# Pooled attention and top-1 experts on one core: softmax guard as a constant column, eleven route steps spread out in place of sixteen, seven low halves on VectorE

## The chip, the cores and the metric

The kernel runs on one core of a Trainium2 chip. The metric is device time in microseconds (us), the median of the runs. Before the change three runs gave 508.53, 511.44 and 512.01 us: median 511.44.

## What is computed

Attention over pooled keys and values, then a mixture of experts on its output. Everything is float32; batch B = 8, heads H = 8, sequence S = 576, head width 64, so 4,608 tokens of width 512; 8 experts of hidden width 1,024.

```python
def attention(q, k, v):                                  # [8, 8, 576, 64] each
    k_p = k.reshape(B, H, 72, 8, D).mean(axis=3)
    v_p = v.reshape(B, H, 72, 8, D).mean(axis=3)
    scores = 1/sqrt(D) * matmul(q, k_p.transpose(0, 1, 3, 2))
    attn = exp(scores - max(scores, axis=-1, keepdims=True))
    attn = attn / (sum(attn, axis=-1, keepdims=True) + 1e-09)
    return matmul(attn, v_p)

def moe(x, w_skip, w_gate, w1, w2):                      # x: [4608, 512]
    out = x.copy()
    xc = x[x @ w_skip > 0]                               # the other tokens keep x
    logits = xc @ w_gate
    e_idx = argmax(logits, axis=1)
    probs = exp(logits - max(logits)); probs /= sum(probs) + 1e-09
    for e in range(8):
        mask = e_idx == e
        out[those tokens] = xc[mask] + gate_w[mask] * (relu(xc[mask] @ w1[e]) @ w2[e])
    return out
```

## The kernel before

**Stages.** The function attention() works through the 36 tiles of 128 tokens in one loop, and while it does so also routes the tokens to their experts. Each token's gate and number go into a table in DRAM that is sorted by expert. slots() reads this table back, and experts() then gathers each expert's tokens, multiplies and writes them. Products are made with float32 split in a high and a low half (hi x hi, lo x hi, hi x lo), for weights as for tokens: ScalarE (ACT) makes a high half (line 558), GpSimd (POOL) the low half as the difference (line 561, 512 columns).

**One tile.** TensorE (PE) makes the scores of two halves of the heads (72 pooled keys for each head), VectorE (DVE) the least (line 279; keys are kept with a negative sign), ACT the exponentials e (line 285), in the next step of the loop PE turns e in five transposes (lines 292 and 293), ACT copies them (line 297), and one step later PE multiplies by the pooled values (lines 310 and 313). A batch's 72 keys of 8 heads don't fill 128 partitions evenly, so 56 or 72 rows of each head go through four transposes, and what is left of all heads, 4 x 16 rows, through the fifth (line 293), against the small value tile vl4 (64 partitions used). The values have 74 columns: 64 of the head, 9 of the values times the gate weights (so that the logits come out of the same matmul), and a column of ones that gives the sum of e. normalised() then takes the tile: line 325 adds 1e-9 to the sum and multiplies by 8, line 327 inverts, line 331 scales the nine logit columns of each head, line 332 scales the values to x, which goes to the output, and line 335 adds the logits over heads into lg. A batch changes every 4.5 tiles. The new batch's keys are added up on DVE (line 185) and its values on POOL (lines 210 to 241), and at the tiles 5, 9, 13, 18, 22, 27 and 31 PE turns the new values: the "turn tiles".

**The route.** After 9, 14, 18, 24, 29, 33 and 36 tiles route() takes the tiles of that group. It is a generator whose steps are DVE instructions on all the group's tiles at once: maximum (353), no token (355), equal (357), difference (359), times expert number (361), maximum (363), plus "no" (365), one-hot r_oh (367). PE then counts, for each token, those before it of the same expert ("ranks", in the PSUM bank mb), ACT takes the exponentials of the differences (371; 378 in the last group), and DVE adds the running offsets (380), picks by the one-hot (381 and 382), adds up and inverts the gates (383 to 385) and makes the row numbers r_di (390). POOL then writes one row per token and tile into the table (line 393, an indirect DMA). After the first group pick() chooses the expert that has most tokens, which is worked on first; after the third, near_tokens() makes the numbers of its first 256 tokens, which are gathered to SBUF (tile ring; line 468) and multiplied by its weights in 48 small product steps during the end of attention and the table's read (lines 507 to 509 and 529 to 531). That expert's weights come in eight chunks during the loop, from tile 15 on.

**What sets the order.** The order in each engine is written out by the program. normal() runs normalised() and takes one route step behind each of its first two instructions. At the end of a tile, queues with budgets are served: dve holds the key sums (0.7 each), act the high halves, and then route steps are taken while DVE's account stays under 1.5, each counted as 0.13. gps serves POOL: low halves (1.25) and table writes (1.27), with work of at least 1.2 between two writes while there is any. Behind the loop normal() runs for the last tiles, the last group's route runs with product steps of the near tokens put between (side()), and slots() computes the experts' places (s_ names), reads the table (line 956), has PE turn the rows and DVE copy them (lines 987 and 988). WROWS is the time that this planner sets for the table's read. The table is filled with "no token" by one DMA from the tile none (line 734) long before.

Of the kernel before, what the change touches and what calls it, by code (L numbers as in the profile page):

```python
# [56 lines left out]
DVE = 1.5  # L57
GPS = 3.2
# [3 lines left out]
WROWS = 3.6  # L62
# [15 lines left out]
KL = SP - KO  # L78

# [20 lines left out]
def emit(tc, q, k, vm, vr, wg, w1, w2, cf, out):  # L100
    nc = tc.nc
    with ExitStack() as top:
# [10 lines left out]
                 pair=cfs[:, 445 + UNITS:].rearrange("p (g h) -> p g h", h=2), next=cfs[:, 445:445 + UNITS], left=cfs[0:4 * KL, 439:443])  # L113
# [14 lines left out]
        none = cp.tile([128, 266], F32, name="none")  # L128
# [20 lines left out]
def attention(tc, nc, q, k, vm, vr, cf, wg, w1, w2, whi, wlo, out, c, pay, offs, table, near, bufs, late, early, mb, fin, cfs):  # L149
    with ExitStack() as ctx:  # L150
# [7 lines left out]
        n4 = 4 * KL  # L158
# [10 lines left out]
        lg = sp.tile([128, NT, 9], F32, name="lg")  # L169
        wide = [sp.tile([128, 128], F32, name=f"ls{i}") for i in range(2)]  # L170
# [21 lines left out]
        def load_v(b):  # L192
# [3 lines left out]
            vl = vp.tile([n4, POOL, HD], F32, name="vl")  # L196
# [4 lines left out]
            nc.sync.dma_start(vl, vr[b])  # L201
# [79 lines left out]
        def exped(e, sc, mn, i):  # L281
            ev = e[:, i].rearrange("p (k g) -> p g k", g=2)
# [5 lines left out]
        def turn_p(e):  # L288
            for i in range(2):
                ev = e[:, i, 2 * KL * i:2 * KL * i + 256].rearrange("p (k g) -> p g k", g=2)  # L290
                for g in range(2):
                    nc.tensor.transpose(ptf[:, (2 * i + g) * 128:(2 * i + g) * 128 + 128], ev[:, g], ident)
            nc.tensor.transpose(ptf[:, 512:640], e.rearrange("p i k -> p (i k)")[:, 256:384], ident)
# [22 lines left out]
        def normalised(t, os):  # L316
            x = ap.tile([128, H, HD], F32, name="x", bufs=5)
            l8 = ap.tile([128, H, 9], F32, name="l8")
            rs = ap.tile([128, 2, 4], F32, name="rs")
# [14 lines left out]
            yield  # L334
# [5 lines left out]
        def route(t0, n):  # L340
# [6 lines left out]
            cube = lambda i: work[:, (4 + i * NE) * GMAX:(4 + i * NE) * GMAX + n * NE].rearrange("p (j e) -> p j e", e=NE)  # L347
            mx, no, se = (col(i) for i in range(3))
            eq, d = (cube(i) for i in range(2))
            r8 = eq  # L350
            cm = new("r_cm"); c2 = new("r_c2"); oh = new("r_oh", NE, dt=BF16)
            ex = new("r_ex", NE); ds = new("r_ds"); di = new("r_di", dt=I32, bufs=4); s2 = new("r_s2")
# [1114 lines left out]
```

## Time and profile before

| | |
|---|---|
| runs: median, lowest, highest | 511.44, 508.53, 512.01 us |
| profiled execution: its own time | 514.2 us |
| its span (first to last instruction) | 512.4 us |
| PE matmuls busy | 476.5 us, 93% of the span |
| PE weight loads busy (beside matmuls) | 431.9 us, 84% |
| DVE busy | 293.6 us, 57% |
| ACT busy | 233.2 us, 46% |
| POOL busy | 218.9 us, 43% |
| moved by DMA | 88.43 MB, mean 173 GB/s |
| granted clock of PE, mean | 0.98 of full speed |

Span and shares are those of the profiled execution, which took 2.8 us longer than the median of the runs. The shares are averages over stages that differ: the setup and key sums (to 38.77 us), the attention loop (to 152.13), the last route and the table's read (to 189.15), and the experts (to the end). A table by stage, or by tile within a stage, says more than the shares. In a timeline each row has start, length, engine, line and operation, the tile written and the tiles read, the shape, and in brackets the idle time of the engine before it with what ended it.

### The profile page before, as it was taken

The numbers are of one execution on the slowest core, as the hardware profiler recorded it, in microseconds if no ns is written. First come the engines' busy times: TensorE is split into PE (matmuls) and PEld (weight loads), VectorE is DVE, ScalarE is ACT, GpSimd is POOL, SyncE is SP. The second block draws the span as 40 slices with busy tenths as digits, with TensorE's granted clock in tenths as the row PEclk, the third lists the DMA queues.
The fourth block names the chain that finished last, engine by engine and source line by source line (L and its number), as shares of the span: only waits on it lengthen the run. The fifth ranks groups of instructions, "written<-read, shape, count | busy, mean of one in ns | idle before, by whom it ended". The sixth has DMA issues, their size and how long they took to land. (4 is left out here: it accounts for less than half of the span.)

```text
span 512.4 us, 10426 instructions
## 1 busy us (share of the span) xinstructions
PE 476.5 (93%) x3155; PEld 431.9 (84%) x3156; DVE 293.6 (57%) x751; ACT 233.2 (46%) x585; POOL 218.9 (43%) x275
## 2 busy tenths in 40 slices
PE   5899899999998598899999998899999999999994
PEld 2789898898898378788989987789899898989893
DVE  4678988988777333468474747752536644222311
ACT  4677678888881012246343626531434442212110
POOL 3578389999984231034302223442032233223221
PEclk9699999999999899999999999999999999999998
DMA  8999899978311039527572555752335111201001
GB/s 255 395 398 378 323 316 375 343 294 265 108 67 43 25 108 340 187 72 262 182 240 93 179 196 175 264 167 73 89 135 173 61 61 36 67 21 58 30 11 39
DMA packets 35364, 88.43 MB, mean 173 GB/s; under 512 B 6770, under 2 KB 9262, under 8 KB 33508
## 3 DMA queue, kind: packets, MB, share of 16 engines
q1 hardware_dynamic: 27104, 71.62, 39.8%
q0 software_dynamic: 8224, 16.39, 9.5%
q8 instruction: 15, 0.25, 0.2%
q14 instruction: 21, 0.17, 0.1%
HBM read 73.58 MB, written 22.05 MB: 187 GB/s over the span
## 5 line engine op out<-in xcount | busy, mean ns | idle before, releaser
L1196 PE MATMUL psl<-xhi,w1hi 128*128 128x256 f32 (+3 forms) x384 | 112.9, 294 | 3.4 <-PEq L1024 2.8
L1197 PE MATMUL psl<-xlo,w1hi 128*128 128x256 f32 (+3 forms) x384 | 112.4, 293 | 0.0
L1198 PE MATMUL psl<-xhi,w1lo 128*128 128x256 f32 (+3 forms) x384 | 112.4, 293 | 0.0
L1111 POOL DMA_INDIRECT out<-ring,slot x36 | 38.3, 1064 | 162.0 <-POOLq L1024 155.7
L1297 ACT ACTIVATE hhi<-psl 128x256 fp32r<-128x256 f32 (+3 forms) x96 | 39.3, 409 | 119.5 <-ACTq L1024 114.8
L1355 DVE SCALAR_TENSOR_TENSOR hlo<-psl,hhi 128x256 fp32r<-128x256 f32 (+2 forms) x96 | 40.4, 422 | 66.4 <-DVEq L1024 61.7
L1196 PEld LDWEIGHTS psl<-xhi,w1hi 128*128 128x128 f32 x384 | 72.1, 188 | 5.1 <-issue 4.7
L1197 PEld LDWEIGHTS psl<-xlo,w1hi 128*128 128x128 f32 x384 | 72.2, 188 | 0.4
L1198 PEld LDWEIGHTS psl<-xhi,w1lo 128*128 128x128 f32 x384 | 72.1, 188 | 0.0
L285 ACT ACTIVATE e<-sc,mn 128x72 f32<-128x72 f32 x288 | 65.1, 342 | 14.5 <-DVE mn L279 14.3
L1287 ACT ACTIVATE xhi<-psd 128x512 fp32r<-128x512 f32 x36 | 19.1, 597 | 80.2 <-ACTq L1024 79.0
L1106 POOL DMA_INDIRECT ring<-out,slot x39 | 42.2, 1083 | 22.6 <-issue 19.0
L310 PE MATMUL o<-vbd,pT 128*128 128x148 f32 (+1 forms) x312 | 49.4, 298 | 2.6 <-DVE x L332 1.6
L393 POOL DMA_INDIRECT table<-pay,r_di x36 | 35.9, 996 | 17.8 <-DVE p_mx L419 7.5
L310 PEld LDWEIGHTS o<-vbd,pT 128*128 128x128 f32 (+1 forms) x312 | 38.6, 179 | 5.6 <-PE mb L376 1.3
L1218 PE MATMUL psf<-w2hi,hhi 128*128 128x512 f32 x96 | 38.0, 396 | 3.4 <-PEq L1024 3.4
L1332 DVE TENSOR_TENSOR w2lo<-stage,w2hi 128x1024 fp32r<-128x1024 f32 x28 | 34.3, 1224 | 8.6 <-DVEq L1024 8.0
L1219 PE MATMUL psf<-w2lo,hhi 128*128 128x512 f32 x96 | 37.4, 390 | 0.0
L1220 PE MATMUL psf<-w2hi,hlo 128*128 128x512 f32 x96 | 37.4, 390 | 0.0
L1105 POOL COPY ring<-gate 128x1 f32<-128x1 f32 x36 | 10.6, 295 | 56.3 <-DMA out<-ring,slot 49.2
L1218 PE MATMUL mb<-w2hi,hhi 128*128 128x512 f32 x88 | 34.3, 390 | 0.0
L1220 PE MATMUL mb<-w2hi,hlo 128*128 128x512 f32 x88 | 34.3, 390 | 0.0
(240 smaller groups left out, 987.9 us busy)
## 6 DMA issues: line engine op xcount, KB each, us to landing
stage<-in_w SPq DMA_DIRECT2D x64, 512.0 KB, 3.7
out<-x SPq DMA_DIRECT2D x36, 256.0 KB
stage<-in_k SPq DMA_DIRECT2D x7, 1152.0 KB
qt<-in_q SPq DMA_DIRECT2D x9, 512.0 KB
hhi<-in_vm SPq DMA_DIRECT2D x4, 1024.0 KB
hlo<-in_vm SPq DMA_DIRECT2D x3, 1024.0 KB
table<-none POOLq DMA_DIRECT2D x1, 2304.0 KB
xhi<-in_q SPq DMA_DIRECT2D x4, 512.0 KB
```

The lines of the kernel that those rows point to most:

```text
L285: nc.scalar.activation(ev[:, h // 2, k0:k0 + SP], sc[:, h * SP:(h + 1) * SP], AF.Exp, bias=mn[:, 4 * i + h:4 * i + h + 1], scale=-1.0)
L310: nc.tensor.matmul(o_[sl, g * 2 * VA:(g + 1) * 2 * VA], pT[:, 2 * a + g, sl], vbd[b % 2][:, 2 * a + g, :], start=(g == 0), stop=False)
L1106: g.indirect_dma_start(ring[:, s % 6, 0:D], None, out, bass.IndirectOffsetOnAxis(ap=slot[:, s:s + 1], axis=0), bounds_check=NTOK - 1, oob_ ...
L1111: g.indirect_dma_start(out, bass.IndirectOffsetOnAxis(ap=offsets, axis=0), ring[:, s % 6, 0:D], None, bounds_check=NTOK - 1, oob_is_err=Fa ...
L1196: t.matmul(ps, whi[0][:, k, w], xhi[:, k, xs], start=(k == 0), stop=False)
L1197: t.matmul(ps, whi[0][:, k, w], xlo[:, k, xs], start=False, stop=False)
L1198: last = t.matmul(ps, wlo[0][:, k, w], xhi[:, k, xs], start=False, stop=(k == 3))
L1218: t.matmul(ps, hhi[:, k, sl], whi[1][:, k, :], start=(k == 0), stop=False)
L1219: t.matmul(ps, hhi[:, k, sl], wlo[1][:, k, :], start=False, stop=False)
L1220: last = t.matmul(ps, hlo[:, k, sl], whi[1][:, k, :], start=False, stop=(k == 7))
L1297: a.activation(hhi[:, f, xs], psL[f % 3][:, xs], AF.Relu).then_inc(sem["act"], 1)
L1355: return v.scalar_tensor_tensor(out[:, f, :], psL[f % 3][:, xs], 0.0, hhi[:, f, xs].bitcast(F32), ALU.max, ALU.subtract)
```

## The change

**The guard.** Each e tile gets 32 more columns between its two halves; the first of them holds 1.0 and the others 0. The fifth transpose takes the columns 256 to 383 as before, so the constant comes out as one row of the turned tile, and the small value tile has 96 used partitions in place of 64, with the value 1e-9 in the sum's column at that row. pair and left, which fill the sum's columns, are multiplied by 8. The sum then comes out of the matmul as 8 (sum + 1e-9), and line 325 is left out of normalised(). The tiles e, vl and ex (the route's exponentials) are fixed buffers, set once by DVE memsets before the loop; the rows of vl come in two DMAs.

**The route.** The one-hot takes six steps in place of eight: equal and times expert number are one scalar_tensor_tensor, and "no" stands in a ninth column of the same tile, so that the maximum takes it in. The running offsets are put into the ranks by a matmul of the identity with offs (line 372), and the copy of the counts back to offs replaces the add. Multiplying by the one-hot and one maximum over nine columns, which makes r_di, replace four steps. The exponentials have a ninth column that holds 1e-9. A step is now counted as 0.24, and from tile 15 on DVE's account for route steps ends at 1.0. In the last group the exponential stands ahead of the ReLU of the near tokens' products on ACT.

**Low halves and the rest.** Of the first expert's sixteen low halves, the second halves of chunks 2 to 6 are made by DVE in the loop (0.65 on its account), and both of chunk 7 by DVE behind the last hidden halves of the near tokens. pick() and near_tokens() take offs and subtract the experts' first rows. The one-element add of line 450 is gone. WROWS is 5.2 in place of 3.6, and the table's fill takes 128 columns of none in place of 256.

```diff
+DVEL = 1.0
...
-WROWS = 3.6
+WROWS = 5.2
...
+GAP = 2 * KL
...
+ebuf = [sp.tile([128, 8 * SP + GAP], F32, name=f"e{i}") for i in range(2)]
+vls = [sp.tile([n4, POOL, HD], F32, name=f"vl{i}") for i in range(2)]
+exps = [sp.tile([128, GMAX, NE + 1], F32, name=f"ex{i}") for i in range(2)]
...
-            nc.sync.dma_start(vl, vr[b])
+            for i in range(2):
+                nc.sync.dma_start(vl[i * 2 * GAP:i * 2 * GAP + GAP], vr[b, i * GAP:i * GAP + GAP])
...
-                nc.vector.tensor_scalar(rs[:, i * n:i * n + n], o[:, :, :, VA - 1], 1e-9, float(POOL), ALU.add, ALU.mult)
-            yield
-            nc.vector.reciprocal(rc, rs)
+                nc.vector.reciprocal(rc[:, i * n:i * n + n], o[:, :, :, VA - 1])
...
-            nc.vector.tensor_tensor(eq, l, bc(mx), ALU.is_equal)
-            yield
             nc.vector.tensor_tensor(d, l, bc(mx), ALU.subtract)
             yield
-            nc.vector.tensor_tensor(eq, eq, epos.unsqueeze(1).broadcast_to([128, n, NE]), ALU.mult)
-            yield
-            nc.vector.tensor_reduce(cm, eq, axis=AX.X, op=ALU.max)
-            yield
-            nc.vector.tensor_tensor(c2, cm, no, ALU.add)
-            yield
-            nc.vector.tensor_tensor(oh, eq, bc(c2), ALU.is_equal)
+            nc.vector.scalar_tensor_tensor(eq, d, 0.0, epos.unsqueeze(1).broadcast_to([128, n, NE]), ALU.is_equal, ALU.mult)
+            yield
+            nc.vector.tensor_reduce(cm, full, axis=AX.X, op=ALU.max)
+            yield
+            nc.vector.tensor_tensor(oh, eq, bc(cm), ALU.is_equal)
             yield NEXT
...
+            nc.tensor.matmul(pr, ident, offs.unsqueeze(1).broadcast_to([128, n + 1, NE]), start=True, stop=False)
...
-            ranked = [lambda: nc.vector.tensor_tensor(r8, pr[:, 0:n], offs.unsqueeze(1).broadcast_to([128, n, NE]), ALU.add),
-                      lambda: nc.vector.tensor_tensor(r8, r8, oh, ALU.mult),
-                      lambda: nc.vector.tensor_reduce(ds, r8, axis=AX.X, op=ALU.add)]
+            ranked = [lambda: nc.vector.tensor_tensor(eq, pr[:, 0:n], oh, ALU.mult),
+                      lambda: nc.vector.tensor_reduce(di, full, axis=AX.X, op=ALU.max)]
             paid = [lambda: nc.vector.tensor_reduce(se, ex, axis=AX.X, op=ALU.add),
-                    lambda: nc.vector.tensor_scalar(s2, se, 1e-9, None, ALU.add),
-                    lambda: nc.vector.reciprocal(pay[:, t0:t0 + n, 1], s2)]
+                    lambda: nc.vector.reciprocal(pay[:, t0:t0 + n, 1], se)]
...
-            nc.vector.tensor_tensor(offs, offs, pr[:, n], ALU.add)
+            fin["counts"] = pr[:, n]
+            if not last:
+                yield
+                nc.vector.tensor_copy(offs, pr[:, n])
...
+        def low_v(cc, i):
+            nc.vector.tensor_tensor(piece(wlo, cc, i), stage[:, room(cc), i * 512:i * 512 + 512],
+                                    piece(whi, cc, i).bitcast(F32), ALU.subtract)
...
         def later_low(cc, i):
+            if cc == 7:
+                return
+            if cc > 1 and i:
+                dve.add(now["t"] + 1, now["t"] + 2, 0.65, lambda: low_v(cc, i))
+                return
             gps.add(now["t"] + 1, (NT if cc > 5 else wload(cc + 3)) - 1, 1.25, lambda: low(cc, i))
...
-                nc.gpsimd.tensor_copy(vbd[i][:, :, (hh + 1) * VA - 1], pair[:, :, hh])
-            nc.gpsimd.tensor_copy(vl4[i][0:n4, :, VA - 1], left)
+                nc.gpsimd.tensor_scalar(vbd[i][:, :, (hh + 1) * VA - 1], pair[:, :, hh], float(POOL), None, ALU.mult)
+            nc.gpsimd.tensor_scalar(vl4[i][0:n4, :, VA - 1], left, float(POOL), None, ALU.mult)
...
-            while t < NT - 1 and busy < DVE and routes.step():
-                busy += 0.13
+            while t < NT - 1 and busy < (DVE if t < PICKED else DVEL) and routes.step():
+                busy += 0.24
...
                 held = kinds(nc.scalar, fin["nti"])
+                for i in range(2):
+                    low_v(7, i)
```

VectorE before, where the second group's route (five tiles) begins in the loop: mn is the least score of a tile, kp the new batch's keys, mb the PSUM bank that also holds the route's work columns.

```order
L185 TENSOR_REDUCE kp<-stage 128x72
L353 TENSOR_REDUCE mb<-lg 128x5
L355 TENSOR_SCALAR mb<-lg 128x5
L357 TENSOR_TENSOR mb<-lg,mb 128x40
L359 TENSOR_TENSOR mb<-lg,mb 128x40
L361 TENSOR_TENSOR mb<-mb,cfs 128x40
L363 TENSOR_REDUCE r_cm<-mb 128x5
L365 TENSOR_TENSOR r_c_1103<-r_cm,mb 128x5
L325 TENSOR_SCALAR rs<-o 128x8
L367 TENSOR_TENSOR r_oh<-mb,r_c_1103 128x40
L327 RECIPROCAL rc<-rs 128x8
```

VectorE after, from the same key sum on (lines 285, 331, 335, 336 and 338 are 279, 327, 331, 332 and 335 of before).

```order
L190 TENSOR_REDUCE kp<-stage 128x72
L356 TENSOR_REDUCE mb<-lg 128x5
L358 TENSOR_SCALAR mb<-lg 128x5
L331 RECIPROCAL rc<-o 128x8
L360 TENSOR_TENSOR mb<-lg,mb 128x40
L335 TENSOR_TENSOR l_1077<-o,rc 128x72
L336 TENSOR_TENSOR x<-o,rc 128x512
L338 TENSOR_REDUCE lg<-l_1077 128x9
L362 SCALAR_TENSOR_TENSOR mb<-mb,cfs 128x5x8
L285 TENSOR_REDUCE mn<-sc 128x4 x2
L190 TENSOR_REDUCE kp<-stage 128x72
L364 TENSOR_REDUCE r_cm<-mb 128x5
```

Of the steps to the one-hot, two stand at the tile's end now, one inside the next tile's normalised(), one behind it and the fifth a tile later, where the first seven of eight stood in a row.

GpSimd before, at the end of the loop and behind it: w2lo is a low half of the first expert's second weights, "table" with r_di a table write, and the last row the table's read (its first rows repeat for some writes ahead of these).

```order
L561 TENSOR_TENSOR w2lo<-stage,w2hi 128x512
L393 DMA table<-pay,r_di 36864x16
L561 TENSOR_TENSOR w2lo<-stage,w2hi 128x512
L393 DMA table<-pay,r_di 36864x16 x9
L956 DMA stage<-table,s_coli 81x2048
```

GpSimd after, at the same place (lines 562, 390 and 974 are 561, 393 and 956 of before; the memset of stage was elsewhere before).

```order
L562 TENSOR_TENSOR w2lo<-stage,w2hi 128x512
L390 DMA table<-pay,r_di 36864x16
L755 MEMSET stage 81x128x2
L390 DMA table<-pay,r_di 36864x16
L562 TENSOR_TENSOR w2lo<-stage,w2hi 128x512
L390 DMA table<-pay,r_di 36864x16 x15
L974 DMA stage<-table,s_coli 81x2048
```

Fifteen writes stand in a row now where nine did, with fewer low halves between the others.

ACT before, behind the loop, where the last group's exponential is (r_ex; lines 837 and 515 make rows of the near tokens' hidden halves).

```order
L837 ACTIVATE hhi<-cfs 128x8x128
L837 ACTIVATE hlo<-cfs 128x8x128
L515 ACTIVATE hhi<-sc 128x2x256
L378 ACTIVATE r_ex<-mb 128x24
L515 ACTIVATE hhi<-pt 128x2x256 x2
```

ACT after, the same place.

```order
L853 ACTIVATE hhi<-cfs 128x8x128
L853 ACTIVATE hlo<-cfs 128x8x128
L378 ACTIVATE ex_130<-mb 128x3x8
L516 ACTIVATE hhi<-sc 128x2x256
L516 ACTIVATE hhi<-pt 128x2x256 x2
```

The exponential of the last group moves ahead of the first hidden half.

## Rows read from the trace of the kernel before

**Rows 1.** Table of two stages: us, busy by engine (instructions), PE clock, DMA share, GB/s
```profile
38.77:152.13 113.36, 109.00 (x912) 102.39 (x911) 97.75 (x357) 92.72 (x307) 95.35 (x105) 1.00 0.78 278
...
189.15:512.40 323.25, 307.72 (x1888) 280.09 (x1888) 153.66 (x259) 113.42 (x190) 87.88 (x107) 0.99 0.38 129
```

**Rows 2.** The same table, between starts of line 332's x on VectorE
```profile
45.36:49.94 4.58, 4.47 (x36) 4.14 (x35) 3.25 (x11) 3.22 (x11) 4.24 (x7) 1.00 1.02 407
...
49.94:53.15 3.21, 3.21 (x27) 3.12 (x26) 2.78 (x10) 2.51 (x9) 0.80 (x1) 1.00 1.07 415
...
53.15:57.60 4.45, 4.16 (x33) 3.87 (x32) 4.21 (x17) 3.47 (x12) 0.24 (x1) 1.00 0.99 394
...
57.60:63.14 5.54, 4.39 (x46) 3.86 (x45) 5.09 (x29) 3.63 (x12) 2.21 (x2) 1.00 0.78 279
...
72.81:77.05 4.24, 4.24 (x35) 4.04 (x34) 4.00 (x17) 3.23 (x12) 2.83 (x4) 1.00 1.01 333
...
88.05:92.23 4.18, 4.18 (x34) 3.87 (x33) 3.94 (x17) 3.88 (x13) 3.82 (x5) 1.00 1.04 401
...
92.23:97.16 4.93, 4.37 (x44) 3.93 (x42) 4.66 (x20) 3.84 (x13) 4.55 (x5) 1.00 1.02 351
...
110.20:119.33 9.13, 8.73 (x74) 8.21 (x72) 8.26 (x35) 7.53 (x25) 8.55 (x14) 1.00 0.59 190
...
128.96:137.54 8.58, 8.49 (x78) 7.88 (x77) 7.23 (x33) 7.14 (x24) 7.92 (x7) 1.00 0.40 124
...
144.14:148.86 4.72, 4.66 (x36) 4.21 (x34) 4.26 (x17) 4.20 (x15) 4.35 (x5) 1.00 0.16 58
```

**Rows 3.** VectorE's timeline in one route burst: start, length, idle before in brackets
```profile
147.30 0.20 DVE L359 TENSOR_TENSOR mb<-lg,mb 128x32 f32<-128x32 f32 x1
147.53 0.20 DVE L361 TENSOR_TENSOR mb<-mb,cfs 128x32 f32<-128x32 f32 x1
...
148.29 0.15 DVE L325 TENSOR_SCALAR rs<-o 128x8 f32<-128x8 f32 x1
148.47 0.20 DVE L327 RECIPROCAL rc<-rs 128x8 f32<-128x8 f32 x1
```

**Rows 4.** Timeline of four engines behind the loop
```profile
156.95 0.18 DVE L367 TENSOR_TENSOR r_oh<-mb,r_c 128x24 bf16<-128x24 f32 x1
...
157.26 0.17 PE L376 MATMUL mb<-r_oh,upper 128*128 128x24 bf16 x1
...
159.50 0.19 ACT L378 ACTIVATE r_ex<-mb 128x24 f32<-128x24 f32 x1
...
159.72 0.19 DVE L380 TENSOR_TENSOR mb<-mb,offs 128x24 f32<-128x24 f32 x1 [2.59 <-ACT r_ex L378]
...
160.79 0.16 DVE L390 TENSOR_TENSOR r_di<-r_ds,mb 128x3 int32<-128x3 f32 x1
...
161.23 0.97 POOL L393 DMA_INDIRECT table<-pay,r_di  x1 [3.56 <-DVE s_n L909]
...
168.40 1.18 POOL L956 DMA_INDIRECT stage<-table,s_coli  x1 [3.65 <-DVE s_last L975]
...
174.63 0.24 DVE L988 CAST slot<-o 128x81 int32<-128x81 f32 x1 [3.44 <-PE o L987]
```

**Rows 5.** Line groups of TensorE in the loop: busy us, mean ns, idle before
```profile
L248 PE MATMUL mb<-wgs,vT 128*128 128x36 f32 x36 | 5.1, 282 | 0.8 <-DVE njt L439 0.8
```

**Rows 6.** Line groups: VectorE's nearest subtraction, GpSimd's low halves (ns minimum/median/maximum)
```profile
L501 DVE TENSOR_TENSOR xlo<-sc,xhi 128x512 fp32r<-128x512 f32 x2 | 1.4, 684 | 0.0
...
L561 POOL TENSOR_TENSOR w2lo<-stage,w2hi x8: 1269/1289/1307, 128.8 to 148.8; 128x512 fp32r<-128x512 f32 x8
```

**Rows 7.** Timeline of GpSimd and VectorE around the one-element add
```profile
95.35 1.28 POOL L561 TENSOR_TENSOR w1lo<-stage,w1hi 128x512 fp32r<-128x512 f32 x1
...
95.45 1.20 DVE L450 TENSOR_TENSOR ncount<-p_cm,p_mx 128x1 f32<-128x1 f32 x1
```

**Rows 8.** GpSimd's timeline: the first table write
```profile
60.91 1.10 POOL L393 DMA_INDIRECT table<-pay,r_di  x1 [7.52 <-DVE p_mx L419]
```

More of the change, by code (lines that the diff above doesn't have):

```diff
@@ L112, in emit @@
         c = dict(ident=cfs[:, 0:128], epos=cfs[:, 384:392], first=cfs[:, 392:400], unit=cfs[:, 436:437], place=cfs[:, 443:444], third=cfs[:, 444:445], wgs=wgs,
-                 pair=cfs[:, 445 + UNITS:].rearrange("p (g h) -> p g h", h=2), next=cfs[:, 445:445 + UNITS], left=cfs[0:4 * KL, 439:443])
+                 pair=cfs[:, 445 + UNITS:].rearrange("p (g h) -> p g h", h=2), next=cfs[:, 445:445 + UNITS], left=cfs[0:4 * KL + GAP, 439:443])
         c["lower"] = cp.tile([128, 128], BF16, name="upper")
@@ L126, in emit @@
                     order=cp.tile([128, NE + 1], I32, name="norder"))
[L128 removed]
+        none = cp.tile([128, 138], F32, name="none")
         stage = cp.tile([128, NST, F], F32, name="stage")
@@ L195, in load_v @@
                 early("room1", 128, 8)
-            vl = vp.tile([n4, POOL, HD], F32, name="vl")
+            vl = vls[b % 2]
             for i in range(2) if b == 0 else ():
@@ L346, in route @@
             col = lambda i: work[:, i * GMAX:i * GMAX + n]
[L347 to L352, printed above, removed]
+            mx, se = (col(i) for i in range(2))
+            full = work[:, 2 * GMAX:2 * GMAX + n * (NE + 1)].rearrange("p (j e) -> p j e", e=NE + 1)
+            eq, no = full[:, :, 0:NE], full[:, :, NE]
+            d = work[:, (3 + NE) * GMAX:(3 + NE) * GMAX + n * NE].rearrange("p (j e) -> p j e", e=NE)
+            cm = new("r_cm"); oh = new("r_oh", NE, dt=BF16); di = new("r_di", dt=I32, bufs=4)
+            ex = exps[list(ends).index(t0 + n) % 2][:, :n]
             nc.vector.tensor_reduce(mx, l, axis=AX.X, op=ALU.max)
@@ L389, in route @@
                 yield
-            nc.vector.tensor_tensor(di, ds, no, ALU.add)
             def write(j):
@@ L440, in pick, with near_tokens @@
             yield
-        def near_tokens(cnt):
+        def near_tokens(ends):
             less = sp.tile([128, 1], F32, name="less")
             nn = sp.tile([128, 1], F32, name="nn")
-            nc.vector.tensor_tensor(p_own, cnt, near["hot"], ALU.mult)
+            nc.vector.tensor_tensor(p_own, ends, c["first"], ALU.subtract)
             yield
-            nc.vector.tensor_reduce(p_cm, p_own, axis=AX.X, op=ALU.add)
+            nc.vector.tensor_tensor(p_own, p_own, near["hot"], ALU.mult)
             yield
-            nc.vector.tensor_tensor(near["count"], p_cm, p_mx, ALU.add)
+            nc.vector.tensor_reduce(near["count"], p_own, axis=AX.X, op=ALU.add)
             yield
@@ L692, in attention @@
             nc.gpsimd.memset(t_, 0.0)
+        for e, vl in zip(ebuf, vls):
+            nc.vector.memset(e[:, 4 * SP:4 * SP + GAP], 0.0)
+            nc.vector.memset(e[:, 4 * SP:4 * SP + 1], 1.0)
+            nc.vector.memset(vl[GAP:2 * GAP], 0.0)
+        for e in exps:
+            nc.vector.memset(e[:, :, NE], 1e-9)
         nc.scalar.activation(near["count"], init[:, 0:1], AF.Exp, scale=0.0)
@@ L757, in normal @@
             routes.step()
-            next(nrm)
+            finish(nrm)
             routes.step()
-            finish(nrm)
             add_routes(t + 1)
@@ L795, in attention @@
             spent = act.take(t, 0.4 if new is not None else 0.0, 1) if t else 0.0
-            es[t] = ap.tile([128, 2, 4 * SP], F32, name="e")
+            es[t] = ebuf[t % 2]
             for i in range(2):
@@ L908, in slots @@
     nc.vector.memset(zero, 0.0)
-    nc.vector.tensor_tensor(n, offs, c["first"], ALU.subtract)
+    nc.vector.tensor_tensor(n, fin["counts"], c["first"], ALU.subtract)
     yield
```

34 lines of the change are left out of this document (18 added, 16 removed).

## The prediction

> **What bounds the kernel now.** I read the table of stages first [rows 1]. The experts fill 323 of 512.4 us with TensorE (PE) busy 307.7, and the change leaves their instructions as they are; what can move is the attention loop (113.4 us in this row) and the 37 us between its end at 152.13 and the experts' first unit at 189.15. In the loop PE, VectorE (DVE), ScalarE (ACT) and GpSimd (POOL) are each busy 82% or more, so shares tell nothing, and I cut it at the starts of DVE's instruction x (line 332), one per tile of 128 tokens [rows 2]. A plain tile takes 3.21 us: PE busy all of it, DVE 2.78. A tile in which a new batch's values are turned takes 4.58 with DVE at 3.25: 1.37 us that DVE doesn't cause. Tiles with route steps are longer: 4.45, 5.54, 4.24, 4.18, 4.93 us, and there DVE's instructions fill the interval while PE shows gaps (4.16 of 4.45, 4.39 of 5.54, 4.37 of 4.93). The route comes as a burst: step starts stand 0.23 us apart (147.30, 147.53) [rows 3], and up to twelve stand in one tile. So PE sets the pace of plain tiles, DVE that of route tiles.
>
> What the eight rows with route steps hold above 3.21 per tile, and above another 1.37 where a turn is in them (5.54, 4.93, 9.13 for two tiles, 8.58 for two), is 1.24 + 0.96 + 1.03 + 0.97 + 0.35 + 1.34 + 0.79 + 1.51 = 8.2 us. That is the most the loop can give by relieving DVE.
>
> Behind the loop a chain sets the end [rows 4]: last group's one-hot (156.95), its ranks on PE (157.26) and exponentials on ACT (159.50), indices (160.79), three table writes on POOL (from 161.23), the read of the table (168.40) that waits for them, and DVE's copy of its rows (174.63). POOL stood idle 3.56 us before those writes, done with the 33 before them at 157.67, so its backlog isn't in this chain.
>
> **Part by part, against the profiled 514.2 us (span 512.4).** The three runs' median is 511.44, so I scale the result by 511.44/514.2.
>
> *Guard through the constant column.* One DVE instruction per tile goes (line 325): about 0.2 us by the starts 148.29 and 148.47 [rows 3]. No matmul is added: the column rides in the leftover transpose, whose tile keeps its 128 columns. The small value tile grows from 64 to 96 partitions at the same elements per partition, which I cost at nothing; the memsets stand ahead of DVE's first data.
>
> *Eleven route steps in place of sixteen, and spread.* I multiplied out DVE's rows between two x of the changed order with the spacings of the trace (0.23 a step, 0.2 less per tile). The first group's two tiles need 3.7 and 3.5, later groups 3.2 per tile with 10 instructions, one tile in which a low half falls 3.5, the tile of the first ring transposes 4.4 (14 instructions). Above 3.21 that leaves 0.5 + 0.3 + 0.1 + 0.3 + 1.2 = 2.4 us of the 8.2; in turning tiles DVE stays under 4.58. Gain 5.8. The upper bound is 8.2; the lower is what PE visibly stood idle in those rows, 0.29 + 1.15 + 0.56 + 0.40 + 0.09 + 0.06 = 2.5. I take 5.8, since PE's ends are modelled and DVE's sums match the lengths.
>
> *Offsets through TensorE.* Each route gains a float32 matmul pair of 80 columns or fewer (line 372) in place of an add. The nearest row is a 36-column float32 matmul: 5.1 us for 36, 0.14 each [rows 5]; two passes in six looped groups are 1.7 us. Nothing if it falls into a PE gap, 1.7 if PE sets the pace everywhere: I take 0.9.
>
> *Seven low halves.* POOL loses seven of 1.28 us, DVE gains seven of about 0.68 (by the nearest DVE subtraction of that size) [rows 6]. Two stand behind the last hidden halves, before DVE waits 3.44 us for the table's rows [rows 4], and are hidden. Five are in the loop; their 0.6 is already in the DVE sums. New is that they read two SBUF tensors while POOL reads SBUF. The trace has one such meeting in the loop: a DVE add of one element took 1.20 us, where small steps take 0.15 to 0.2 [rows 3], and ended as a POOL low half ended [rows 7]. (The change removes that add.) So each may wait 0 to 1.28 us; I take 0.6 on average, 0.4 at the three where DVE has no slack: 1.2, between 0 and 5 x 1.28 = 6.4.
>
> [...]
>
> POOL afterwards: first write about 1.3 us earlier (the first group's indices by the sums above), seven halves at 1.24 us of spacing gone, 1.3 more for writes that now stand next to each other. The 33rd write would end at 157.67 - 1.3 - 8.7 + 1.3 = 149, 152 if each of five DVE halves holds POOL up. The last group's indices come near 155, so fifteen writes in a row stay hidden by 3 us or more. Had the seven halves stayed, POOL would end near 156.4 and its last three writes would be late by 1 us: that is what moving them buys here.
>
> *Table fill of 512-byte rows in place of 1 KB.* POOL stood idle 7.52 us before its first table write [rows 8], so some microseconds more in making or landing the fill are covered.
>
> *Tail.* Before the last indices DVE loses one guard step (0.2), two steps before the one-hot (0.4) and, net, two behind the ranks (0.4): 1.0 us. The 2.59 us between the one-hot and the next DVE step are odd: PE's ranks are recorded done at 157.43, yet ACT's exponential, which DVE waited for, starts at 159.50 [rows 4]. Before, ACT has a ReLU of the near-token products ahead of it; in the changed order the exponential comes first. Between 0 and 2.0 may go; I take 1.0. Behind the indices all waits are the same, and the experts too. WROWS changes nothing: in both orders 36 of 48 product steps precede the table's transposes, the limit.
>
> Sum: 5.8 - 0.9 - 1.2 + 1.0 + 1.0 = 5.7 us; 514.2 - 5.7 = 508.5, scaled 505.8 us.
>
> **Rivals.**
> 1. *PE paces it all.* Rows such as 4.18 us with PE busy 4.18 speak for it; that PE has 27 matmuls in a plain tile's row and only seven more in that one, most of them small, speaks against. The loop gives 2.5 and pays 0.9 and 1.2: 514.2 - 2.4 = 511.8, scaled 509.0 us.
> 2. *Both waits vanish.* The halves meet no POOL read that matters, and the last exponential is prompt: 5.8 - 0.9 + 1.0 + 2.0 = 7.9 us less, scaled 503.6. For it: the new ACT order; against: [rows 7].
> 3. *The halves starve (slower).* If POOL's next read takes the interface again each time, a half on DVE waits not for one POOL instruction but until POOL issues a write. The changed order has one run of about 12 us without a write (from the sixth w1 half left on POOL to the near-token gathers), and two of the five halves fall at it. Waiting 6 us each, they cost 12 in place of 0.8: 514.2 - 5.7 + 11.2 = 519.7, scaled 516.9. It decides the sign from 6.9 us of extra waiting on. Against it: the one-element add got in after a single POOL instruction; but a write, not a read, came next there.
>
> **How the numbers follow.** Forecast 0.55, rival 1 0.18, rival 2 0.19, rival 3 0.08. A measurement of this kernel can tell about 1% from no change; 1% below 511.44 is 506.3. The forecast's own range, 503.5 to 508, lies about two thirds below that: 0.55 x 0.68 + 0.19 = 0.56 faster; rival 3 and a little of rival 1, 0.09 slower; 0.35 within 1%. The range for eight in ten is 501 (all bounds but one good) to 510.5 (rival 1 with dear halves).
>
> **What would show it.** Right: intervals between two x with route steps near 3.2 to 3.5 us, no tile but the first ring tile above 4.6, the last x of the loop near 148.5 us in place of 152.13, POOL idle before the last three writes. DVE's five 512-column halves between 0.68 and 1.9 us long. Wrong: intervals as long as before with PE busy in them (rival 1), a DVE half of 3 us or more (rival 3), a last group's first write that starts where the twelfth of the row ends (POOL bound after all), or an expert stage that isn't 323 us.

## The result and the profile after

The changed kernel takes 506.01 us (503.58 to 508.87, 14 runs), the kernel before 511.46 us (508.53 to 513.77, 14 runs) on the same chip: a ratio of 0.9901, 95% interval 0.988 to 0.9923. The forecast was 505.8. The profiled execution has a span of 504.2 us, with PE busy 475.2, DVE 288.5, ACT 232.8 and POOL 212.8.

The table of stages between starts of x, now line 336, in the columns of [rows 1]. The first two rows are a turn tile and a plain one, the last is the first ring tile (the first that also turns gathered tokens), and the others hold route steps.

```profile
44.34:48.92 4.58, 4.52 (x37) 4.14 (x36) 3.09 (x11) 3.23 (x11) 3.63 (x6) 1.00 1.02 387
48.92:52.13 3.21, 3.21 (x28) 3.12 (x27) 2.64 (x9) 2.53 (x9) 0.60 (x1) 1.00 1.05 359
...
55.64:59.72 4.08, 3.59 (x37) 3.38 (x37) 3.48 (x18) 3.31 (x12) 0.75 (x1) 1.00 1.02 411
...
77.36:82.83 5.47, 5.15 (x45) 4.62 (x44) 3.46 (x15) 4.06 (x13) 5.11 (x7) 1.00 1.02 379
92.45:97.87 5.42, 5.11 (x52) 4.56 (x51) 3.44 (x15) 4.05 (x13) 5.20 (x6) 1.00 1.04 416
97.87:102.30 4.43, 4.34 (x35) 4.03 (x33) 4.39 (x12) 3.91 (x12) 4.07 (x5) 1.00 0.86 320
116.49:120.42 3.93, 3.93 (x38) 3.74 (x37) 3.70 (x12) 3.03 (x11) 3.85 (x6) 1.00 0.56 194
141.73:146.64 4.91, 4.84 (x38) 4.39 (x36) 4.36 (x15) 4.40 (x15) 3.69 (x5) 1.00 0.17 58
```

Against [rows 2]: plain and turn tiles are as long as before, and the bursts of 4.2 to 5.5 us are gone. But two turn tiles now last 5.47 and 5.42 us, one tile 4.43 with DVE busy throughout, and one 3.93 with PE busy throughout.

The timeline behind the loop, the counterpart of [rows 4]:

```profile
153.11 0.18 DVE L366 TENSOR_TENSOR r_oh<-mb,r_cm 128x24 bf16<-128x24 f32 x1
...
153.67 0.17 PE L376 MATMUL mb<-r_oh,upper 128*128 128x24 bf16 x1
...
153.88 0.19 ACT L378 ACTIVATE ex<-mb 128x24 f32<-128x24 f32 x1 [3.93 <-PE mb L376]
...
154.11 0.19 DVE L380 TENSOR_TENSOR mb<-mb,r_oh 128x24 f32<-128x24 f32 x1 [0.81 <-ACT ex L378]
...
154.56 0.19 DVE L381 TENSOR_REDUCE r_di<-mb 128x3 int32<-128x27 f32 x1
...
155.11 0.97 POOL L390 DMA_INDIRECT table<-pay,r_di  x1 [1.14 <-DVE s_own L929]
...
160.80 1.08 POOL L974 DMA_INDIRECT stage<-table,s_coli  x1 [2.17 <-DVE s_odd L985]
...
166.86 0.24 DVE L1006 CAST slot<-o 128x81 int32<-128x81 f32 x1 [0.94 <-PE o L1005]
```

The 2.59 us between one-hot and next DVE step are 0.81 (whether the change did that is a question for experiment 3); POOL still stands idle (1.14 us) before its last three writes; the read follows the first write by 5.69 us (7.17 before).

Both kernels were traced twice (the second traces are two of the experiments below). This table splits the span at starts of instructions in those traces, as differences; the forecast column sorts the prediction's terms into the same stretches.

| stretch, us | before | after | forecast | mean change |
|---|---|---|---|---|
| start to the first x | 23.82, 22.68 | 23.00, 22.44 | 0 | -0.5 |
| first to 35th x (the loop) | 128.31, 128.39 | 126.65, 125.65 | -3.7 | -2.2 |
| to the last one-hot | 4.82, 4.92 | 3.46, 3.46 | -0.6 | -1.4 |
| to the last row numbers | 3.84, 3.83 | 1.45, 1.45 | -1.4 | -2.4 |
| to the table's read | 7.61, 6.98 | 6.24, 6.25 | 0 | -1.0 |
| to the slots' copy | 6.23, 6.20 | 6.06, 6.09 | 0 | -0.1 |
| to the experts' first unit | 14.52, 14.26 | 13.08, 13.55 | 0 | -1.1 |
| to the end | 323.27, 324.88 | 324.26, 325.69 | 0 | +0.9 |

The loop repeats to 0.08 us in the kernel before; in the changed kernel it differs by 1.00 us, by the one tile whose subtraction took 1.75 us in the first trace and 0.74 in the second (experiments 1 and 7). Between the two traces of a kernel the start differs by 1.14 and 0.56 us and the experts by 1.61 and 1.43. The traces' sum, -7.9, is more than the runs' -5.45, and outside their interval (-3.9 to -6.1). So not every difference in this table is one of the runs. The record names no chip for the first trace of the kernel before: its execution took 514.2 us, more than any of the 14 runs beside the changed kernel. Its second trace is of another chip (experiment 1).

### The profile page after: what moved, and what is told of

Same layout as the page of the kernel before. It is cut to its first block, busy times and chain, and to the rows that moved or that the text cites. A ratio compares the mean times of both kernels' runs of the same rounds, so it can differ in the third digit from the quotient of the medians.

```text
span 504.2 us, 10440 instructions
## 1 busy us (share of the span) xinstructions
PE 475.2 (94%) x3169; PEld 431.9 (86%) x3170; DVE 288.5 (57%) x695; ACT 232.8 (46%) x585; POOL 212.8 (42%) x268
## 5 line engine op out<-in xcount | busy, mean ns | idle before, releaser
L1123 POOL COPY ring<-gate 128x1 f32<-128x1 f32 x36 | 12.2, 340 | 54.6 <-DMA out<-ring,slot 48.3
L285 DVE TENSOR_REDUCE mn<-sc 128x4 f32<-128x288 f32 x72 | 30.7, 454 | 7.0 <-PE sc L279 4.9
L1237 PE MATMUL mb<-w2lo,hhi 128*128 128x512 f32 x88 | 34.3, 390 | 0.0
```

The source lines that it names most:

```text
L1237: t.matmul(ps, hhi[:, k, sl], wlo[1][:, k, :], start=False, stop=False)
```

## The experiments

Each was timed against the kernel before on the same chip, but the chips differ. The second trace of the kernel before and the experiments 2, 5 and 6 are of chip 0, where the kernel before takes 515.22 us; the others are of the chips 12, 13 and 14, where it takes 510.55 to 511.1. For chip 0 the record has no run of the changed kernel. "The sum" is what the 27 tiles from the fourth start of x to the 31st hold above 3.21 us (4.58 in the six turn tiles among them): 7.14 and 7.21 in the two traces of the kernel before.

**1. Both kernels again.** No edit.

> The changed kernel once more, as the base for the three beside it and for a second trace. Theory A (what its first trace shows): x of the 35th tile starts near 149.7 us; the tile behind the third group's row numbers is 4.4 us long because the subtraction of the experts' first rows, two SBUF operands, waits 1.5 us behind GpSimd; ranks cost TensorE 0.7 to 0.9 us in each of five tiles; the product steps between the table's read and the first expert run at full clock. Time 506 us, ratio to the kernel before 0.990. Rival B: part of the 8.2 us between the two first traces is chance (the 1.0 us in the start, the clock in the tail); then this trace has its first x near 23.8 us in place of 23.0, or a clock of 0.5 in the tail, and the ratio is nearer to 0.993.

> The kernel before once more, for a second trace. Theory A: the loop's tiles have the same lengths to a hundredth of a us (7.1 us above 3.21 and 4.58 in the tiles 6 to 32); the start (23.82 us to the first x) and the granted clock behind the table's read are what differs between executions: the clock was 0.5 from 174.5 to 181.3 us in the first trace and may be 0.5 for as long here. Rival: that fall of the clock was chance and is missing here; then the stretch from the slots' copy to the first expert is some 2 us shorter than 14.5 us.

Measured: the changed kernel 506.08 us, ratio 0.9898 (0.9872 to 0.9924). The kernel before, on chip 0 where its other runs had a median of 515.22 us, took 515.5 us, ratio 1.0004 (0.9975 to 1.0033). The sum is 5.71 in the first trace of the changed kernel and 4.71 in the second, the difference being one tile (4.43 against 3.43 us). The stages from the slots' copy to the first unit, one row each of before_again and after_again:

```profile
173.00:187.26 14.26, 11.71 (x49) 9.29 (x49) 4.04 (x8) 1.80 (x3) 5.30 (x6) 0.80 0.25 72
```
```profile
165.34:178.89 13.55, 11.44 (x49) 9.03 (x49) 3.72 (x8) 1.80 (x3) 5.32 (x6) 0.87 0.26 77
```

The same 49 PE instructions ran at a mean granted clock of 0.80 and 0.87. Before, PE had its product steps done early and stood idle 2.87 and 2.14 us ahead of the table's transposes; in the changed kernel that gap is 0.60 and 0.61 us, because the table's read comes 7.6 us earlier and the last of the products ahead of the gap ends only 5.5 to 6.0 us earlier. Later, where PE has waited within the first unit (3.11 us, to 197.36, in the first trace), the clock is low in the changed kernel too: 0.84 on the mean from 193 to 204 us in the first trace and 0.72 here.

```profile
192.00:204.00 12.00, 8.59 (x30) 6.80 (x29) 5.75 (x8) 4.35 (x6) 0.00 (x0) 0.72 0.67 235
```

(In the second trace of before it is low there as well, 0.74 from 204 to 208 us; in the first it stays at 1.00 behind a wait of 3.40 us.) Behind the table's read the clock is low in both traces of the kernel before, 0.77 and 0.80, against 1.00 and 0.87 after, and 0.77 again in the kernel of experiment 3, where the gap is 1.33 us. What lowers it no run shows. What it is worth, some 1.1 us, may in part be given back in the experts, whose 324 us differ by up to 1.6 us between traces of one kernel, so that this can't be told.

**2. The constant column alone**, put into the kernel before (every other part as there).

> The kernel before with the constant column alone: line 325 leaves the tile, all route steps, budgets and low halves stay. Theory A: some ten tiles of the loop are DVE-bound and become 0.2 us shorter each, the plain ones stay at 3.21: the sum above 3.21 and 4.58 falls from 7.1 to 5.1; behind the loop one instruction less and the 0.77 us wait ahead of it may go: 1.0 us. Together 2 to 3 us: near 508.5 us, ratio 0.995. Rival: the route's burst is bound by something else than DVE's count (the ranks on TensorE), and one instruction less changes nothing: 511 us.

Measured: 513.35 against 515.22 us, ratio 0.9954 (0.9927 to 0.9981); the sum 5.93, the loop 1.7 us shorter (126.63) and the stretch to the last one-hot 1.1. Theory A holds, smaller in the loop than it said; 0.8 of the 1.1 is the wait ahead of the last halves of x, which is missing in the kernel of experiment 3 too. By the traces this loop is as long as that of the whole change (126.65 and 125.65; 126.34 in experiment 4): in the loop the constant column alone gives most of what the change gives.

**3. The seven low halves alone**, put into the kernel before.

> The kernel before with the seven low halves alone moved to VectorE (five in the loop, two behind the last hidden halves). Theory A: alone this buys nothing, since before GpSimd was idle 3.56 us ahead of the last writes and its backlog not in the chain; VectorE gets five halves of 0.68 us and some waits behind GpSimd of up to 1.3 us, in tiles of which two or three are bound by VectorE already: 0 to 2 us slower, 511 to 513 us if the kernel before takes 511 (ratio 1.000 to 1.004). The 3 us that the halves are worth in the changed kernel come only where the last group's row numbers are ready earlier. Rival: GpSimd's reads hold up others in the loop too (one-element steps, the pooled sums), and taking seven halves off it is worth 2 to 3 us by itself: ratio 0.995.

Measured: 511.62 against 510.55 us, ratio 1.001 (0.9986 to 1.0034); the sum 7.83. By themselves they buy nothing that can be measured.

This trace also tells something of the tail. Up to the table's read the order behind the loop is that of the kernel before: the ranks stand behind 27 of PE's products, and ACT makes a ReLU of the first 24 of these (line 515) and only then the last exponential (line 378). The last of the 24 and ACT, first in the kernel before, then here, with DVE's step behind the one-hot and POOL's read:

```profile
155.47 0.28 PE L509 MATMUL sc<-xhi,w1lo 128*128 128x256 f32 x1
159.01 0.60 ACT L515 ACTIVATE hhi<-sc 128x512 fp32r<-128x512 f32 x1 [6.84 <-remote]
```
```profile
157.24 0.28 PE L509 MATMUL sc<-xhi,w1lo 128*128 128x256 f32 x1
157.56 0.60 ACT L515 ACTIVATE hhi<-sc 128x512 fp32r<-128x512 f32 x1 [4.23 <-PE sc L509]
158.40 0.19 ACT L378 ACTIVATE r_ex<-mb 128x24 f32<-128x24 f32 x1 [0.25 <-PE mb L376]
158.62 0.19 DVE L380 TENSOR_TENSOR mb<-mb,offs 128x24 f32<-128x24 f32 x1 [0.56 <-ACT r_ex L378]
165.84 1.08 POOL L967 DMA_INDIRECT stage<-table,s_coli  x1 [2.18 <-DVE s_short L974]
```

In the kernel before ACT starts 3.26 us behind the recorded end of that product, here 0.04. So the wait behind the one-hot is 0.56 us with the old order of ACT, less than the 0.81 of the changed kernel. To the one-hot, the row numbers and the read this kernel takes 3.98, 1.82 and 6.14 us (the changed one 3.46, 1.45 and 6.25), together 11.94, where the two traces of the kernel before have 16.0 on the mean. If the kernel before took 16.0 here in its runs too, this kernel, whose loop is 1.3 us longer by the traces, would gain more than 2 us on it. By the ratio it loses 0.5 (from a gain of 0.7 to a loss of 1.7). So the 4.1 us belong to those two traces, or to their chip, and not to the order.

**4. The low halves taken back** out of the changed kernel.

```diff
 def later_low(cc, i):
-    if cc == 7:
-        return
-    if cc > 1 and i:
-        dve.add(now["t"] + 1, now["t"] + 2, 0.65, lambda: low_v(cc, i))
-        return
     gps.add(...)
...
-                for i in range(2):
-                    low_v(7, i)
```

> The changed kernel with all sixteen low halves on GpSimd again, the seven that VectorE makes among them. Theory A: GpSimd is then 8.7 us longer at work, has some 5 us of idle time in the loop's last quarter to take it, and ends its row of writes 2 to 3 us behind the moment at which the last group's row numbers are ready; the table's read comes 1 to 3 us later: 507 to 509 us. My forecast had 1 us for it. Rival (the halves on VectorE cost the loop as much as they save behind it, by the shared SBUF access): the loop ends 1 us earlier and the time is 505 to 506 us.

Measured: 509.05 us, ratio 0.996 (0.994 to 0.9981), 3.0 us more than the changed kernel beside it. DVE's last row numbers and two of POOL's writes, timeline of this kernel:

```profile
155.42 0.18 DVE L381 TENSOR_REDUCE r_di<-mb 128x3 int32<-128x27 f32 x1
```
```profile
156.70 0.98 POOL L390 DMA_INDIRECT table<-pay,r_di  x1 [0.30 <-issue]
157.99 0.97 POOL L390 DMA_INDIRECT table<-pay,r_di  x1 [0.31 <-DVE s_units L941]
```

The last group's first write (157.99) follows the one before it without a pause, 2.57 us behind its row numbers: POOL's backlog is in the chain, as theory A said. Experiments 3 and 4 together show a part that is worth nothing alone and 3 us beside the others. Without it the other parts reach a ratio of 0.996, no better than the constant column alone (0.9954, on another chip).

**5. The bursts back**, with eleven steps.

```diff
-while t < NT - 1 and busy < (DVE if t < PICKED else DVEL) and routes.step():
-    busy += 0.24
+while t < NT - 1 and busy < DVE and routes.step():
+    busy += 0.13
```

> The changed kernel with the budgets of before for route steps (0.13 a step, 1.5 throughout), so that the eleven steps come in a burst again. Theory A: a tile with six steps holds 13 VectorE instructions and lasts 3.9 to 4.1 us, the next one holds five steps and the ranks; each of five groups loses 0.5 to 0.8 us: the sum over tiles 6 to 32 is 7 to 8.5 us in place of 4.7, and the time 508 to 510 us. Rival: the ranks on TensorE (0.7 to 0.9 us in one tile of each group) hide the burst, spreading buys nothing and the time stays at 506.

Measured: 513.49 against 515.22 us, ratio 0.9962 (0.9941 to 0.9984), 3 us less of a gain than the changed kernel has on other chips. But the sum is 5.28, not 7 to 8.5, and within the changed kernel's 4.71 to 5.71: the tiles with six steps last 3.8 to 4.0 us as expected, but most of the ranks' tiles behind them are then shorter. In these tiles the rival holds: spreading buys nothing. What is longer is the first ring tile, 9.03 us in place of 4.91, and the tile behind it, 4.56 in place of 3.00. Near theory A on the ratio, then, and not on the place. PE and DVE in the first ring tile:

```profile
145.89 0.41 PE L320 MATMUL o<-vl,pT 128*128 128x148 f32 x2
149.02 0.63 PE L499 MATMUL sc<-cfs,ring 128*128 128x128 f32 x4 [2.71 <-issue]
```
```profile
147.50 0.82 DVE L285 TENSOR_REDUCE mn<-sc 128x4 f32<-128x288 f32 x2 [4.61 <-PE o L320]
```

PE's matmul is recorded as ended at 146.3, DVE and ACT get its signal only at 147.5, and PE goes on at 149.02. The profile names nothing that it waited for. Experiment 6, whose steps are spread, has the same two tiles at 10.70 and 4.56 us on the same chip, so these 5.7 us are not shown to be the bursts' work (last section). What spreading is worth, this run doesn't tell.

**6. The offsets added by DVE again**, twelve steps and no line 372.

> The changed kernel with the offsets added by VectorE again (twelve steps, no float32 matmul of the identity with the offsets). Theory A: TensorE sets the pace in the ranks' tiles, so each loses 0.25 us (the two passes start 0.11 to 0.14 apart): the sum over tiles 6 to 32 falls from 4.7 to about 3.7, VectorE's step more is hidden there, and costs 0.2 us behind the last ranks: near 505.2 us. My forecast put the matmuls at 0.9 us in all. Rival: VectorE's additional step costs what the matmul did: 506 us or more.

Measured: 512.13 against 515.22 us, ratio 0.9931 (0.9907 to 0.9956), whose interval overlaps the changed kernel's from other chips: no gain is shown. This trace too has late signals of PE in the first ring tile (10.70 us), and a low half of 3.03 us on DVE that made a tile 2.29 us longer than in the changed kernel. The matmul's cost isn't isolated by this run.

**7. The counts from PSUM**: the two subtractions of the experts' first rows no longer have two SBUF operands.

```diff
-yield from pick(offs)
+yield from pick(pr[:, n])
...
-yield from near_tokens(offs)
+yield from near_tokens(pr[:, n])
```

> The changed kernel, with the counts read from the PSUM bank (where the ranks' matmul leaves them) in place of the SBUF copy, in the two first steps behind the first and the third group, so that neither has two SBUF operands. Theory A: the subtraction of 1.75 us falls to 0.2 us, the tile of 4.43 us to 3.0 to 3.3, and the loop ends 1.2 us earlier; time 1.2 us less than the changed kernel (near 504.8). Rival: the step waited for the PSUM bank or for its own result, not for GpSimd's use of SBUF; then it stays above 1 us and the time stays at 506.

The changed kernel at this place:

```profile
99.66 0.99 POOL L390 DMA_INDIRECT table<-pay,r_di  x1 [0.17 <-DVE mn L285]
...
100.26 1.75 DVE L447 TENSOR_TENSOR mb<-offs,cfs 128x8 f32<-128x8 f32 x1
...
100.67 1.29 POOL L216 TENSOR_TENSOR hlo<-hlo 128x512 f32<-128x512 f32 x1
```

It began during a table write, did not get in between the write and the pooled sum 20 ns later, and ended (102.01) with the sum. With the counts from PSUM, line 447 took 0.165 us and the tile 3.20. That the second SBUF operand made the wait is shown, and the rival is out; that GpSimd held it up is read from the times above. The time was 506.2 us, ratio 0.9907 (0.9881 to 0.9933): no gain, also because the step took only 0.745 us in the second trace of the changed kernel, beside which it ran.

**8. The exponentials a tile earlier.**

```diff
-            yield NEXT
             last = t0 + n == NT
             if not last:
                 nc.scalar.activation(ex[:, :, 0:NE], d, AF.Exp)
+            yield NEXT
```

> The changed kernel, with the route's exponentials issued on ScalarE right behind the one-hot, a tile earlier, in place of just ahead of the ranks. Theory A: TensorE's first rank matmul waits 0.3 to 0.5 us for them in each of three or four tiles (0.29 in both tiles of 5.4 us) and the attention exponentials behind them start 0.9 us late; without it the two tiles of 5.47 and 5.42 us fall to 4.8 to 5.1 and the loop ends 0.8 to 1.5 us earlier: near 505 us. Rival: those tiles are long because of the rank matmuls alone (0.4 us) and the turn, whoever they wait for; then they stay above 5.3 us and the time stays at 506.

Measured: the tiles of 5.47 and 5.42 us became 4.99 and 4.95, as theory A said. But the tile behind the first ring tile grew by 0.87 us, and the time was 507.16 us, ratio 0.992 (0.9894 to 0.9946): no gain.

**9. Both, and two ways around a waiting half.** "best" joins 7 and 8 (8 without the sixth group); "best_six" leaves one more half to POOL; "best_late_half" makes that half a tile later.

```diff
 best_six:       -if cc > 1 and i:
                 +if cc > 2 and i:
 best_late_half: -dve.add(now["t"] + 1, now["t"] + 2, ...)
                 +dve.add(now["t"] + 1 + (cc == 2), now["t"] + 2 + (cc == 2), ...)
```

> The changed kernel with the counts read from PSUM in the two steps behind the first and third group, and the route's exponentials issued a tile earlier in the groups of 14, 18, 24 and 29 tiles (not in the sixth, where it lengthened the tile behind the first ring tile by 0.87 us; the first group gets it too). Theory A: tiles of 5.47 and 5.42 us become 5.0 us, no wait of the subtraction, all else as in the changed kernel: the sum over tiles 6 to 32 is 3.6 to 3.8 us in place of 4.7 to 5.7 and the time 1 to 2 us less than the changed kernel's, ratio 0.986 to 0.988. Rival: what the loop saves is taken back behind it, by the clock or by waiting for the gathers, and the ratio stays at 0.990.

> The version with the counts from PSUM and the earlier exponentials, and with six low halves on VectorE in place of seven: the one that took 2.90 us there (chunk 2) is GpSimd's again. Theory A: the tile that was 2.36 us too long becomes plain (0.0 to 0.2), GpSimd has 1.3 us more to do in the loop's middle, which its idle time before the last low half takes up; the loop ends 2 us earlier than with seven: ratio 0.984 to 0.987. Rival: the wait moves to the next half or step that meets GpSimd there, or GpSimd's row of writes ends behind the last row numbers by 0.7 us or more, and the ratio stays at 0.989.

> The same version with seven halves, the one of chunk 2 a tile later, where a low half and the small steps of the near tokens' places stand on GpSimd. Theory A: what a half waits is set by what GpSimd does at that moment: its length is between 0.7 and 3 us and can't be told from the orders of the two engines alone; if it is under 1.4 us the tiles 23 and 24 are 0.4 us too long together in place of 2.36, ratio 0.984 to 0.987. Rival: the first half waits for something of its own (its data), and takes 2.9 us a tile later as well.

Measured: best 506.34 us, ratio 0.9889 (0.9845 to 0.9932). The tiles that 7 and 8 are about are shorter as expected, and one tile is 2.36 us too long, where the first low half on DVE met POOL (timeline of best):

```profile
104.75 0.99 POOL L392 DMA_INDIRECT table<-pay,r_di  x1 [0.17 <-DMA xlo<-in_q]
105.27 2.90 DVE L568 TENSOR_TENSOR w1lo<-stage,w1hi 128x512 fp32r<-128x512 f32 x1
105.75 0.64 POOL L225 TENSOR_TENSOR vl<-ls,cfs 96x256 f32<-96x256 f32 x1
106.32 1.29 POOL L564 TENSOR_TENSOR w1lo<-stage,w1hi 128x512 fp32r<-128x512 f32 x1
107.78 1.27 POOL L392 DMA_INDIRECT table<-pay,r_di  x1 [0.17 <-issue]
```

It began in a write, lasted through two POOL instructions that followed without a pause, and ended (108.17) 0.56 us behind the second of them, in the next write, which lasted longer in turn (1.27 in place of 0.99). That it got in at POOL's pause of 0.17 us is read from these times. In best_six (504.71 us, ratio 0.9878, 0.9854 to 0.9903) that tile is plain, but the next half is 2.16 us long and its tile is 0.93 us longer: the wait moved in part. It is the fastest version that was run; its interval overlaps the changed kernel's. best_late_half took 511.06 us, ratio 0.9994 (0.9972 to 1.0016): here the half first waits for a load of weights.

```profile
114.00 1.75 DVE L568 TENSOR_TENSOR w1lo<-stage,w1hi 128x512 fp32r<-128x512 f32 x1 [4.88 <-DMA stage<-in_w]
```

DVE and everything behind it stood 4.88 us, the tile took 9.2 us, and the whole gain was lost by moving one instruction by one tile.

## Why the prediction was right, step by step

The total was right to 0.2 us, the parts were not, so that much agreement is luck. The loop gave 2.2 us by the traces in place of 3.7. The stretch from there to the last row numbers gave 3.8 in place of 2.0 against the two traces of the kernel before, but 0.9 against experiment 3, which has the order of before. Between the slots and the first unit, where nothing was forecast, 1.1 us went. With the 0.9 these are 4.2 us, inside the runs' interval of 3.9 to 6.1; the rest of the 5.45 stays open. Rival 1 came true for some tiles; of rival 2 the cheap halves came nearly true, and its 2.0 us for a prompt exponential is not shown. Of the signs that the prediction named, the halves' lengths, POOL's idle time before the last writes and the loop's end (149.65 and 148.09) came; "no tile but the first ring tile above 4.6" failed (5.47, 5.42 and, in a third turn tile, 4.79).

- *PE sets the pace of plain tiles, DVE that of route tiles.* Right; plain tiles stayed 3.21 us, and one instruction less in each tile shortened route tiles alone (experiment 2).
- *Eleven steps, spread: 5.8 us.* The step that failed is "above 3.21 that leaves 2.4 us": it multiplied out DVE alone, and left PE's ranks out. The ranks of five groups make one tile each 0.66 to 0.89 us longer (4.08, 5.47, 5.42, 3.93, 3.87 us, two of them turn tiles), and PE is busy 3.93 of 3.93 in one of them. With the steps in bursts most of these tiles are shorter (experiment 5). This is rival 1, true for one tile of each group: with all terms in, the loop gave 2.2 us of the 3.7 forecast, and the constant column gives 1.7 alone (experiment 2). What fewer steps and their spreading are worth by themselves no run shows.
- *Offsets: 0.9 us.* The two passes start 0.13 to 0.17 us apart in six of the seven groups of the first trace, 0.04 in the other (0.14 estimated). Their cost was not isolated.
- *Seven low halves: 1.2 us of waits.* In the two traces of the changed kernel the five halves of the loop took 0.68 to 1.34 us, 0.26 and 0.95 us of waiting in all, next to none of it in a tile's length. But a half that lasts through more than one POOL instruction, as rival 3 has it, exists: 2.90 us (best) and 3.03 us (experiment 6) where a half met three POOL instructions in a row (not the 6 us of rival 3). The interface that rival 3 speaks of was the author's guess; the traces show lengths alone. The order of the changed kernel escaped it, and nothing in the forecast could tell which orders do.
- *A wait that the prediction missed.* It counted the one-element add of [rows 7] as removed and didn't see that the change puts a subtraction of two SBUF tensors in nearly the same place: 1.75 and 0.74 us there.
- *POOL's backlog: 1 us late if the halves had stayed.* Right in kind, 2.57 us by the trace and 3.0 us by the times (experiment 4). The writes stayed hidden behind the last row numbers, by 1.1 us and not 3.
- *Tail: 1.0 + 1.0 us.* The 1.0 for fewer instructions is right: 0.9 against experiment 3 (0.5 to the one-hot, 0.4 behind it). The step that failed is the wait, "Between 0 and 2.0 may go; I take 1.0". The traces show 2.59 and 2.57 before and 0.81 after, but experiment 3, with the ReLU still ahead of the exponential, waits 0.56. So the order on ACT did not make the 2.59, and nothing is shown to be gained by changing it.
- *"Behind the indices all waits are the same, and the experts too."* Wrong: the read waits for the last write's landing (its semaphore's last update is at 167.37 us in the first trace before and 159.78 in the first after, and the read starts 1.03 and 1.02 us behind it), and POOL's idle time ahead of it is 2.17 us in place of 3.65 [rows 4] and 3.03 (second trace). But experiment 3 has 2.18 with the old order, so this is not shown to be a gain either. The 1.1 us between the slots and the first unit went with the granted clock (0.77 and 0.80, then 1.00 and 0.87); experiment 3, at 0.77, takes 14.86 us there.

## What to carry to other kernels

Before spreading work out of a burst, add up every engine for the tiles in which it lands: what the burst covered can be the next bound (here the ranks on PE, which is busy 3.93 of 3.93 us in one tile). Before a wait in a trace goes into a forecast, look for it in the trace of a kernel with the same order on another chip: the 2.59 us of this one were 0.56 there. A part can be worth nothing alone and 3 us beside others, so test it both ways, put in alone and taken out alone. VectorE instructions with two SBUF operands among dense GpSimd work had no fixed length here (0.68 to 3.03 us for a half of 512 columns, 0.74 to 1.75 us for the subtraction of line 447, and 0.165 us for that one with an operand in PSUM): try such an operand in PSUM if that is free, and look at the trace of each new order.

## What the runs showed that was not expected

In five traces (both of the kernel before, and experiments 2, 5 and 6) PE's signals reach the other engines 0.9 to 4.4 us behind the recorded end of its matmul, at places that repeat in both traces of the kernel before (0.90 and 3.26 us in the first of them); in the other nine there are none. In before the two places are the 0.77 and 2.59 us waits behind the loop [rows 4]; in experiment 2 DVE waits there even longer (its timeline):

```profile
158.78 0.19 DVE L383 TENSOR_TENSOR mb<-mb,offs 128x24 f32<-128x24 f32 x1 [4.93 <-ACT r_ex L381]
```

In the same five traces 17 to 22 of some 188 records of PE's semaphore are missing (22 in the first trace of the kernel before), in the others at most one. Four of the five were taken on chip 0 and no other trace was. For the fifth, the first trace of the kernel before, no chip is on record; its 514.2 us lie among the runs on chip 0 (511.61 to 518.48). So the chip explains these traces at least as well as the kernel does: experiment 3, the nearest to the kernel before, has no late signal on chip 13, and the kernel before takes some 4 us more on chip 0 than elsewhere, as its traces there have 4.1 us more behind the loop than experiment 3. The changed kernel on chip 0 would tell, and was not run.

What makes PE's signals late in these traces, and records go missing in them, no run shows. Whether PE is late only while it is profiled stays open: by its trace experiment 2 gains 0.5 us up to the last row numbers, by its ratio 2.4.
